# Loading W2 by row blocks and summing the left half of the first MLP's second product for three tiles at once

## The chip, the cores and the metric

The kernel runs on one core of one Trainium2 chip. The metric is the device time of one launch in microseconds (us): the median of the runs of a kernel. The profile is one execution more, recorded with its own time; the span in the profile runs from the first instruction of the program to the end of the last.

The engines are named as the profile names them: PE (matrix products; PEld its weight loads), DVE (vector work), ACT (activations), POOL (general elementwise work; it also issues the DMAs that change the type on the way) and SP (issues DMAs only).

## The reference

Attention with RMS-normed queries and keys over 8 batches, 12 heads, 448 tokens and 64 columns a head, then an MLP with LayerNorm and a residual on the joined heads. Cut to what is computed:

```python
q_n, k_n = rmsnorm(q, g_q), rmsnorm(k, g_k)              # (8, 12, 448, 64)
attn = softmax(q_n @ k_n.transpose(0, 1, 3, 2) / 8)
x = (attn @ v).transpose(0, 2, 1, 3).reshape(8, 448, 768)
xn = (x - mean(x)) / sqrt(var(x) + 1e-6) * g_ln
out = x + maximum(xn @ w_ch1, 0) @ w_ch2                 # w_ch1 (768, 3072), w_ch2 (3072, 768)
```

All inputs and the output are float32. The kernel multiplies in float16 with float32 sums.

## The kernel before

**Tiling.** Attention goes by pairs of heads (48 pairs, six a batch), each in seven steps of up to 128 keys: `scores` (L394) makes a product in PSUM and an exponential on ACT, `values` (L438) multiplies the exponentials by V. Work ahead of a pair (squares, roots, scaling, splitting K into a high and a low part, transposing) is done by `pieces` (L233) for a unit of one or two pairs. Units from `DMA_UNIT = 7` on are transposed by DMA: `dma_k` (L303) and `dma_q` (L309) on SP; the earlier ones on PE.

The MLP of batch b runs while the attention of batch b+1 does, on the same engines. `run_rest` (L976) takes the pieces of the MLP in order; each has a cost in columns, and after each piece, and after its first half, `upto` emits attention steps up to the same share of the batch's attention. So the order of instructions on each engine is fixed when the program is built: every engine works its own queue in order, and waits where an operand isn't there.

**Batch 0's MLP** is `first_mlp` (L708). The first product makes 24 row blocks of 128 hidden columns (`up`, one PSUM bank each, Relu on ACT into `hS`). The second is `down(t, g, s)`: for token tile t (three of 128 tokens), column half g of W2 (0 is the left 384 columns, 1 the right) and s from 0 to 7, three matmuls each, over row blocks 3s to 3s+2 of W2. A yield takes two values of s, so each (t, g) is four pieces of six matmuls, and the whole product 24 pieces, 144 matmuls of 128x384. A sum lives in one bank of the pool `ps_m` (tag "mlp", three banks, which the first product uses too) from s = 0 to s = 7; then `add` (L754) on DVE scales it by the LayerNorm factor and adds it to x. Before the change the order is g, then t, then s: one sum at a time.

**W2** stands in SBUF as `sh.w2[128, 24, 768]`: row block f of W2 in the second index. `load_w2(g)` (L611) fetches it on POOL's queue, float32 in memory and float16 in SBUF. Before the change g names a column half: the left half in one DMA, the right half in two DMAs of 12 row blocks each. `W2_AT = 47, 71` says at which steps of the attention they are issued. In front of the second call a POOL instruction copies one column of `kU` into `rr`, a place that `least` (L433) writes again afterwards. It reads what the transposing DMA of unit 7 writes (`dma_k`, step 70), so POOL waits for that transpose before it issues the rest of W2. The rows of V for units from 7 on (`load_v`, L207) are issued on the same queue, some between the two calls and some behind the second.

The part of `sh.w2` that row blocks 0 to 7 take holds V of batch 0 until POOL has copied it (`v_first`, L162); row blocks 12 to 23 hold nothing before W2 comes.

**After batch 0**, `weight_sums` (L760) makes differences of the quarters of W2 on DVE (L763) for the later batches. The first of them are emitted after the pieces of batch 0 of which fewer than ten are left.

Of the kernel before, what the change touches and what calls it, by code (L numbers as in the profile page):

```python
# [8 lines left out]
FP32 = mybir.dt.float32  # L9
# [7 lines left out]
ts = bass.ts  # L17
# [3 lines left out]
NDC, NFF = DM // 128, FF // 128  # L21
# [44 lines left out]
HALF, HCOL = NFF // 2, DM // 2  # L66
# [25 lines left out]
class _Fast:  # L92
# [518 lines left out]
    def load_w2(self, g):  # L611
        if g:
            self.nc.gpsimd.tensor_copy(out=self.rr[:, DMA_UNIT:DMA_UNIT + 1],
                                       in_=self.kU[DMA_UNIT % 2][:, 0:1])
        for c in (slice(0, HALF), slice(HALF, NFF)) if g else (slice(0, NFF),):
            self.nc.gpsimd.dma_start(
                out=self.sh.w2[:, c, ts(g, 384)],
                in_=self.w2[128 * c.start:128 * c.stop, ts(g, 384)].rearrange("(c p) d -> p c d", p=128))

    def tok_tiles(self, b):  # L620
        x = self.xs[b]
# [86 lines left out]
    def first_mlp(self):  # L708

        nc, sh = self.nc, self.sh  # L710
        tiles, xnT, hT, cur = self.tok_tiles(0), self.xnT, self.hS, {}

        def up(f, i):
            if i == 0:
                cur["h"] = self.ps_m.tile([128, 512], FP32, tag="mlp", name="psH")
            ps = cur["h"]
            for dc in range(3 * i, 3 * i + 3):
                nc.tensor.matmul(ps[:, 0:384], sh.w1[:, dc, ts(f, 128)], xnT[:, dc],
                                 start=(dc == 0), stop=(dc == NDC - 1))
            if i:  # L720
                nc.scalar.activation(out=hT[:, f], in_=ps[:, 0:384], func=AFT.Relu)

        def down(t, g, s):
            if s == 0:
                cur["ps"] = self.ps_m.tile([128, 512], FP32, tag="mlp", name="psC")
            ps = cur["ps"][:, 0:HCOL]
            for f in range(3 * s, 3 * s + 3):
                nc.tensor.matmul(ps, hT[:, f, ts(t, 128)], sh.w2[:, f, ts(g, HCOL)],
                                 start=(f == 0), stop=(f == NFF - 1))
            if s == 7:  # L730
                self.add(0, t, g, ps)
                if g and t < 2:
                    self.late.append((0, t, slice(0, DM)))
                elif t == 2 and not g:
                    self.late.append((0, t, slice(0, HCOL)))
                elif t == 2:
                    self.store(0, t, slice(HCOL, DM))
            elif s == 3:
                self.store_late()

        for f in range(UP_FIRST, NFF):
            yield 6 * 384 / 2.4, [lambda f=f, i=i: up(f, i) for i in range(2)]
        for g in range(2):
            for t in range(3):
                for s in range(4):
                    yield 6 * HCOL / 2.4, [lambda t=t, g=g, s=s: down(t, g, s)
                                           for s in (2 * s, 2 * s + 1)]

    def store_late(self):
        for a in self.late:  # L750
# [500 lines left out]
```

## Time and profile before

| what | us |
|---|---|
| median of 3 runs (581.79 to 582.78) | 582.78 |
| the profiled execution's own time | 579.58 |
| span of the profile | 578.0 |
| PE busy | 559.5 (97%) |
| DVE busy | 381.7 (66%) |
| ACT busy | 364.4 (63%) |
| POOL busy | 207.0 (36%) |
| first product of batch 0 on PE (L718) | starts 56.3 to 87.9 |
| second product of batch 0 on PE (L728) | starts 88.3 to 118.2 |

The profiled execution took 3.2 us less than the median of the runs, and its span is 1.6 us shorter than its time. Busy times are unions over the whole span; a row of PE shows a matmul from its issue to its modelled end, so two in a row overlap, and the distance between starts is what PE needs for one. In lists of instructions in order of time the columns are start, length, engine, line, operation, what it writes and reads, and the count of the instructions that were merged into the row; in brackets, where there is one, the idle time of the engine before it and what ended it. "q0" is the DMA queue on which POOL issues, "q1" the one on which SP does; their rows give packets, MB as landed, and the time that their packets took as a share of 16 DMA engines.

### The profile page before, as it was taken

To read this page: it belongs to the slowest core of one execution; us is meant where nothing else is said; L and a number is where in the kernel's file an instruction comes from. 1 tells how busy PE (TensorE), PEld (TensorE's weight loads), DVE (VectorE), ACT (ScalarE), POOL (GpSimd) and SP (SyncE) were. 2 spreads that over 40 slices of the span, in tenths; PEclk is the share of its full clock that TensorE was granted. 3 is DMA by queue.
4 is the path that set the end of the run, shared out by engine and by line. 5 is a ranking of instruction groups with operands and counts; after the bars stand their busy time and mean duration, and the time that the engine had idled before them with its cause. 6 is when DMAs were issued, how large, how long until landed. Compare 5 with 4: busy or idle time off the path is not lost.

```text
span 578.0 us, 13670 instructions
## 1 busy us (share of the span) xinstructions
PE 559.5 (97%) x5446; PEld 411.9 (71%) x5446; DVE 381.7 (66%) x826; ACT 364.4 (63%) x674; POOL 207.0 (36%) x224
## 2 busy tenths in 40 slices
PE   5788999999999999999999999999999999999997
PEld 4556666687686867777677768777777777878684
DVE  6989567699657586845667586854756743664424
ACT  5998787447675779557775588637777477323130
POOL 5885636404440620654241521644242320020000
PEclk9999999999999999999999999999999999999999
DMA  8999999958672876969663798958743390030201
GB/s 206 251 238 222 214 207 165 193 147 137 124 131 77 158 127 145 127 148 121 121 106 48 184 134 136 128 143 122 145 64 65 119 113 1 1 110 1 83 2 58
DMA packets 178329, 72.59 MB, mean 126 GB/s; under 512 B 138212, under 2 KB 173220, under 8 KB 178260
## 3 DMA queue, kind: packets, MB, share of 16 engines
q1 hardware_dynamic: 133876, 52.52, 44.1%
q0 software_dynamic: 43440, 18.52, 25.2%
q8 instruction: 44, 0.72, 0.5%
q10 hardware_dynamic: 944, 0.62, 0.4%
q14 instruction: 25, 0.20, 0.1%
HBM read 52.76 MB, written 11.01 MB: 110 GB/s over the span
## 4 chain that ended last, share of the span: by engine, by line
PE 77%; DVE 1%; issue 0%; DVEq 0%
PE psH L798 33%; PE psP L821 30%; PE psS L405 7%; PE oA L458 4%; PE oB L460 1%; PE psS L411 1%; DVE qn L83 0%; DVE w2s L763 0%; DVE ssq L265 0%; DVE w L763 0%; DVE xn L662 0%; DVE hS L804 0%; DVE x L475 0%; DVE xl L757 0%; DVE xl L480 0%
## 5 line engine op out<-in xcount | busy, mean ns | idle before, releaser
L421 ACT ACTIVATE E<-psS,rr_all 128x448 f16<-128x448 f32 x336 | 204.6, 634 | 47.3 <-PE psS L405 40.3
L798 PE MATMUL psH<-xnT,w 128*128 128x256 f16 (+1 forms) x2016 | 225.7, 261 | 0.0
L798 PEld LDWEIGHTS <-w 128*128 128x128 f16 x2016 | 172.8, 98 | 24.3 <-issue 4.9
L801 ACT ACTIVATE hS<-psH 128x512 f16<-128x512 f32 x150 | 89.8, 599 | 97.2 <-PE psH L798 93.0
L821 PEld LDWEIGHTS <-hS 128*128 128x128 f16 x1080 | 100.0, 98 | 57.3 <-issue 1.1
L821 PE MATMUL psP<-w,hS 128*128 128x384 f16 x672 | 127.0, 326 | 0.0
L405 PE MATMUL psS<-qU,kU 128*128 128x448 f16 x288 | 100.9, 352 | 5.0 <-ACT E L421 3.2
L458 PEld LDWEIGHTS <-E 128*128 128x128 f16 x1008 | 70.3, 98 | 35.8 <-issue 2.8
L279 POOL TENSOR_TENSOR k<-k,gprod 128x896 f32<-128x896 f32 x18 | 38.9, 2160 | 139.5 <-ACT khl L259 113.2
L804 DVE TENSOR_TENSOR hS<-hS 128x512 f16<-128x512 f16 (+1 forms) x119 | 60.2, 512 | 19.3 <-ACT hS L801 17.8
L821 PE MATMUL psP<-w2s,hS 128*128 128x384 f16 (+1 forms) x408 | 69.9, 321 | 0.0
L458 PE MATMUL oA<-v,E 128*128 128x65 f16 x864 | 66.9, 193 | 1.1 <-ACT E L421 0.6
L757 DVE SCALAR_TENSOR_TENSOR x<-psP,rs_all,x 128x384 f32<-128x384 f32 x60 | 36.4, 617 | 42.4 <-PE psP L821 41.8
L460 PE MATMUL oB<-v,E 128*128 128x65 f16 x288 | 52.0, 193 | 0.1
L832 POOL TENSOR_TENSOR x<-x,hS 128x384 f32<-128x384 f32 x21 | 23.4, 1126 | 76.1 <-ACT hS L900 75.5
L473 DVE RECIPROCAL rec_all<-oA 128x6 f32<-128x6 f32 x48 | 9.2, 193 | 53.6 <-PE oA L458 53.5
L216 POOL DMA_DIRECT2D v<-in_v_dram x54 | 41.5, 781 | 4.0 <-PE oB L460 2.7
L405 PEld LDWEIGHTS <-kU 128*128 128x128 f16 x288 | 28.0, 98 | 11.1 <-issue 2.2
L900 ACT ACTIVATE hS<-hS,rs_all 128x384 f32<-128x384 f32 x27 | 14.6, 604 | 33.0 <-DVE hS L804 33.0
L460 PEld LDWEIGHTS <-E 128*128 128x128 f16 x336 | 32.4, 96 | 0.4 <-DVE xl L480 0.3
L83 DVE SCALAR_TENSOR_TENSOR qn<-q,rr_all 128x256 f16<-128x256 f32 (+2 forms) x69 | 24.8, 420 | 7.2 <-ACT rr_all L269 7.1
L265 DVE TENSOR_REDUCE ssq<-khl 128x14 f32<-128x896 f32 (+1 forms) x24 | 25.5, 1061 | 5.0 <-ACT khl L259 4.8
(145 smaller groups left out, 616.6 us busy)
## 6 DMA issues: line engine op xcount, KB each, us to landing
k<-in_k_dram SPq DMA_DIRECT2D x19, 384.0 KB, 4.2
q<-in_q_dram SPq DMA_DIRECT2D x18, 384.0 KB, 3.9
out_dram<-x SPq DMA_DIRECT2D x14, 384.0 KB, 3.0
w<-in_moe_w_ch_dram POOLq DMA_DIRECT2D x3, 1536.0 KB, 14.3
v<-in_v_dram POOLq DMA_DIRECT2D x54, 64.0 KB, 4.4
out_dram<-x POOLq DMA_DIRECT2D x9, 384.0 KB, 2.7
w<-in_moe_w_ch_dram POOLq DMA_DIRECT2D x1, 2304.0 KB, 22.5
w<-in_moe_w_ch_dram POOLq DMA_DIRECT2D x2, 1152.0 KB, 14.4
```

The source lines that it names most:

```text
L216: nc.gpsimd.dma_start(out[:, :, j, 0:D], main[:, :, j])
L265: nc.vector.tensor_reduce(out=c["ssq"][:, n], in_=c["sq", n], axis=AX.X, op=ALU.add)
L279: (nc.vector if u in DVE_KG else nc.gpsimd).tensor_tensor(out=c["t"][1], in0=c["t"][1], in1=sh.gprod.unsqueeze(1).broadcast_to([128, g, D] ...
L405: nc.tensor.matmul(ps[0][:, 0:S], c["main"][:, ts(i, 128)], c["q"][:, ts(h, S)], start=True, stop=True)
L421: nc.scalar.activation(out=o, in_=x[:, 0:S], func=AFT.Exp, scale=self.units[u][3][:, g:g + 1], bias=EXP_BIAS)
L458: nc.tensor.matmul(oA[:, t, cs], E[:, ts(t, 128)], rhs, start=(i == 0 and t == 0), stop=(i == 6 and t == 2))
L460: nc.tensor.matmul(oB[:, cs], E[:, 320:448], rhs, start=(i == 0), stop=(i == 6))
L757: self.nc.vector.scalar_tensor_tensor(out=x, in0=ps, scalar=self.rs[:, b, t:t + 1], in1=x, op0=ALU.mult, op1=ALU.add)
L798: nc.tensor.matmul(ps[:, i], sh.w1[:, dc, ts(f + i, 128)], self.xnT[:, dc, 256 - N:256], start=(i == 0 and dc == 0), stop=(i == k - 1 and ...
L801: nc.scalar.activation(out=hT[:, f:f + k], in_=ps, func=AFT.Relu)
L804: nc.vector.tensor_tensor(out=out, in0=a, in1=c, op=op)
L821: nc.tensor.matmul(bank[x][:, c], a[:, f], w[:, f, c], start=(start and f == 0), stop=(stop and f == HALF - 1))
```

## The change

`load_w2(0)` now fetches row blocks 0 to 11 of W2 in all 768 columns, in two DMAs of six row blocks; `load_w2(1)` fetches row blocks 12 to 23 in the same way, still behind the copy that waits for unit 7's transpose. There were three DMAs and are four; the bytes are the same, and a row of a DMA is 768 columns where it was 384.

The left half (g = 0) of batch 0's second product runs with s outside and t inside: two values of s for tile 0, 1 and 2, then the next two. Three sums are open at once, so `cur` is keyed by t. The right half (g = 1) keeps its order: tile by tile, with all s for each.

```diff
-        for c in (slice(0, HALF), slice(HALF, NFF)) if g else (slice(0, NFF),):
+        for c in (0, 6) if not g else (12, 18):
             self.nc.gpsimd.dma_start(
-                out=self.sh.w2[:, c, ts(g, 384)],
-                in_=self.w2[128 * c.start:128 * c.stop, ts(g, 384)].rearrange("(c p) d -> p c d", p=128))
+                out=self.sh.w2[:, c:c + 6],
+                in_=self.w2[128 * c:128 * c + 768].rearrange("(c p) d -> p c d", p=128))
...
         def down(t, g, s):
             if s == 0:
-                cur["ps"] = self.ps_m.tile([128, 512], FP32, tag="mlp", name="psC")
-            ps = cur["ps"][:, 0:HCOL]
+                cur[t] = self.ps_m.tile([128, 512], FP32, tag="mlp", name="psC")
+            ps = cur[t][:, 0:HCOL]
...
-        for g in range(2):
-            for t in range(3):
-                for s in range(4):
-                    yield 6 * HCOL / 2.4, [lambda t=t, g=g, s=s: down(t, g, s)
-                                           for s in (2 * s, 2 * s + 1)]
+        for g, s, t in ([(0, s, t) for s in range(4) for t in range(3)]
+                        + [(1, s, t) for t in range(3) for s in range(4)]):
+            yield 6 * HCOL / 2.4, [lambda t=t, g=g, s=s: down(t, g, s)
+                                   for s in (2 * s, 2 * s + 1)]
```

## The prediction

> **What bounds the kernel now.** I read the page first, then the PE waits, then PE's and POOL's rows in order of time around batch 0's second product, then the DMA queues in short windows. The page's chain of waits, by engine:
>
> ```profile
> PE 77%; DVE 1%; issue 0%; DVEq 0%
> ```
>
> PE holds most of the chain. The view of who waited for whom, PE alone, from 60 us to the end, lists two waits and nothing else:
>
> ```profile
> PE tr L382 <- DVE kU L373: 0.3, 1, 0.3
> PE psS L405 <- ACT E L421: 0.3, 1, 0.3
> ```
>
> One late stretch in the busy-time view (length, then PE, PEld, DVE, ACT, POOL busy, granted clock, DMA share, GB/s):
>
> ```profile
> 200.00:400.00 200.00, 200.00 (x1967) 149.43 (x1966) 134.95 (x297) 137.33 (x253) 78.84 (x84) 1.00 0.81 130
> ```
>
> So after 60 us PE has no slack worth naming, and a wait put into PE there moves the end by its own length: nothing later can give it back. The change acts between 61 and 118 us. What PE does there, from the rows in order of time (start, length, line, count):
>
> ```profile
> 88.33 0.65 PE L728 MATMUL psC<-w,hS 128*128 128x384 f16 x3
> ...
> 97.58 1.14 PE L728 MATMUL psC<-w,hS 128*128 128x384 f16 x6
> ...
> 100.74 1.14 PE L728 MATMUL psC<-w,hS 128*128 128x384 f16 x6
> ```
>
> L728 is the second product: 24 pieces of 6 matmuls, one every 0.163 us when nothing is between. Counting the rows from 88.33, piece 7 begins with the first matmul at 97.58, piece 10 with the fourth at 100.74 (101.23), piece 13 at 105.5, and piece 15 at 108.6 (in a row of 66 matmuls that starts at 107.62). Before, piece 13 is the first to read the right half of W2. When W2 comes, from POOL's rows:
>
> ```profile
> 61.42 1.51 POOL L616 DMA_DIRECT2D w<-in_moe_w_ch_dram  x1
> ...
> 87.33 0.18 POOL L613 CAST rr_all<-kU 128x1 f32<-128x1 f16 x1 [8.04 <-DMA kU<-khl]
> 87.57 2.09 POOL L616 DMA_DIRECT2D w<-in_moe_w_ch_dram  x2
> ```
>
> and L616's times from issue to landing (min, median, max of three):
>
> ```profile
> DMA to landing us min/median/max: 10.9/17.8/22.5
> ```
>
> The 22.5 is the whole left half: 83.9, 4.4 us ahead of 88.33. The 10.9 belongs to the DMA issued at 87.57 (landed 98.5), the 17.8 to the one some 1.03 later (106.4). Before, those are rows 0-11 of the right half, wanted at 105.5, and rows 12-23, wanted at piece 15 (108.6): 7 and 2.2 us to spare. The gate in front of them is L613, which copies one column of unit 7's transposed K and so waits for that transpose.
>
> **The change, part by part.**
>
> *PE's work*: 144 matmuls of the same shape and as many weight loads, the same yields, the same order of attention between them: 0. *Order*: the left half now runs through row blocks 0-5 for three tiles, then 6-11, 12-17, 18-23. Blocks 12-17 are therefore wanted at piece 7 (97.58) and 18-23 at piece 10 (101.23). They are the two DMAs behind the gate. With the old landings (98.5 and 106.4) PE would wait 0.9 us, then until 106.4: 5.2 us in all. What is left of this depends on how much sooner whole rows land.
>
> *Rows of 1536 landed bytes for 768.* Packets, MB and share of each queue, in 98.5 to 101 us, where the W2 queue is alone; in 101 to 104, where SP's q and k loads run beside it; and in 44 to 48, where W1, whose rows land as 2048 bytes, runs beside SP's loads:
>
> ```profile
> q0 software_dynamic: 655, 0.50, 131.9%
> ```
> ```profile
> q0 software_dynamic: 468, 0.36, 76.1%
> q1 hardware_dynamic: 442, 0.34, 45.1%
> ```
> ```profile
> q0 software_dynamic: 321, 0.66, 86.3%
> q1 hardware_dynamic: 323, 0.25, 24.6%
> ```
>
> Shared, the queues go row for row whatever the sizes (468 to 442, 321 to 323), so a wider row takes a larger share. A pair of rows costs an engine 16 x 3/468 = 0.103 us with 768, 16 x 4/321 = 0.199 with 2048; on the line between them 0.161 with 1536: 0.153 MB/us where it had 0.36/3 = 0.120. Alone, 655 rows in 2.5 us are 0.201 MB/us; for wider rows the bounds are that (no gain) and, with the same slope, 0.061 + 0.058 = 0.119 us a row, 0.206 MB/us. I take 0.206, for W1's pair has the slope in it; it hardly matters.
>
> [...]
>
> *The gate.* Unit 7's transpose is issued at 80.69 behind its last operand on DVE, not behind a load, and landed 6.6 us later. Its line, over all units:
>
> ```profile
> DMA to landing us min/median/max: 4.0/5.6/8.0
> ```
>
> W2's first load should be through sooner: between 66 and 80 us the W2 queue moved 2273 rows beside 2269 on SP's queue. So unit 7's small V rows, behind it, clear the engines before the transpose's packets come. Bounds for the gate: 87.33 as now, and 80.69 + 4.0 = 84.7. I take the median, 86.3: 1.0 us sooner.
>
> *The two DMAs behind it*, 1.18 MB each. Before: 1410 rows by 97 us, 1045 more by 101. The first DMA's 1536 rows were through at 97.5, and it landed 1.0 later; the last 617 at 156 per us were through at 104.95, and it landed 1.45 later. From 92 to 97.2 it ran at 1056/5.2 = 203 rows per us, not 262, beside SP's transposes: 1.2 us lost, of which wide rows win back between 0 and all; I take 0.6. After: first DMA through at 97.5 - 1.0 - 0.6 = 95.9, landed 96.9: piece 7 doesn't wait, with 0.7 us to spare. Second: alone to 101.0, 5.1 x 0.206 = 1.05 MB, the other 0.13 at 0.153 takes 0.85, so 101.85 + 1.45 = 103.3. Piece 10 waits 103.3 - 101.2 = **2.1 us**. Late end: gate unmoved, nothing won back, 0.201: 3.5 us alone, 0.70 MB, 0.48/0.153 = 3.1, landed 105.55, stall 4.3. Early end: gate 84.7, all 1.2 won: landed before 101.2, stall 0.
>
> *POOL's issues.* 3072 rows cost 1.51 us, 1536 rows 1.03: 0.81 each for 768 on that line, at most 1.06. First load 1.62 for 1.51, second 1.62 for 2.09. Behind the first stand unit 6's casts and L290, and then POOL idles 3.8 us until 73.78: 0, and 0.1 to 0.6 if somebody waited for those casts; nobody does in the view of waits. SP issues nothing new; its q and k loads land a little later, wanted by ACT at 105.6 at the soonest.
>
> *Three sums at once* take all three banks of the pool psH used. The third sum's bank is freed by ACT's last Relu (88.22 + 0.49), its piece comes near 91. Adds (0.62 each on DVE) move from 94, 101 and 105.7 to about 105 to 107, where DVE was idle; the right half's first sum wants the first bank two pieces later. 0; without that cover 0.6 per add. Weight sums (L763) start at 111.64 as before, plus the stall.
>
> **Sum.** Everything is 0 but the stall: span 578.0 + 2.1 = 580.1; this execution 579.6 + 2.1 = 581.7. It lies 3.2 below the median of the runs, so the forecast goes on the median: 582.8 + 2.1 = **584.9**.
>
> **Rivals.**
>
> *Whole rows arrive in time.* It decides from a landing of the fourth DMA at 102.4 or sooner (stall under 1.2). For it: the gate could come 2.6 us sooner, and each microsecond of it moves up to 0.206 MB out of the stretch that SP's loads share, which is worth 1.3 us of landing. Against: the median of L306 gives 1.0 only. Time 582.8, 582.8 to 584.0. Chance 0.20, of which 0.06 ends below by scatter (the runs shown span 1.0 us).
>
> *Wide rows bring nothing.* The fourth DMA lands at 106.4 as now: stall 5.2, time 588.0. For it: alone the queue may be limited by bytes, 0.201 against 0.206. Against: the row-for-row sharing. PE's clock then matters. At the end PE idles with the clock still granted:
>
> ```profile
> 574.20:578.00 3.80, 0.00 (x0) 0.00 (x0) 0.42 (x1) 0.00 (x0) 0.00 (x0) 1.00 0.51 159
> ```
>
> so 3.8 us idle cost nothing. Cold, the same warm-up matmul ran at half speed:
>
> ```profile
> 5.98 2.74 PE L532 MATMUL psW<-id 128*128 128x128 f16 x24
> ...
> 9.29 0.72 PE L532 MATMUL psW<-id 128*128 128x128 f16 x10
> ```
>
> from 2.74 to about 8.7 us, so a fall costs at most 3.0 more: 588 to 591. Chance 0.13. [...]
>
> *A bank isn't free.* The adds queue up on DVE and PE waits for a bank at piece 13: up to 3 x 0.62 = 1.9 more, 586.8. Chance 0.03; DVE is busy 0.5 of 4.3 us there.
>
> **The numbers.** Forecast, stall 1.2 to 4.3 (584.0 to 587.1): 0.64. Faster or slower by over 0.2% (1.2 us) is what a measurement here can tell from none: faster 0.06, same 0.14, slower 0.64 + 0.13 + 0.03 = 0.80. Range 582.4 to 588.6: it holds the forecast, most of the first rival and the plain 5.2 us stall, and leaves out the fall of the clock.
>
> **What would show it.** PE's L728 with an idle of about 2 us before one matmul near 101 to 103.5, released by a DMA of w; no wait at piece 7; L613 near 86.3; W2's third and fourth DMA landing near 97 and 103.3; PE unbroken after it. No such wait on L728 means the first rival; a landing at 106 the second; a stall with an unmoved span would break the premise that PE has no slack.

## The result and the profile after

| | before | after |
|---|---|---|
| median of 10 runs, us | 581.89 | 584.96 |
| runs, us | 581.58 to 582.78 | 582.58 to 586.74 |
| ratio, 95% interval | | 1.0048 [1.0033, 1.0063] |
| the profiled execution's own time, us | 579.58 | 585.00 |
| span of the profile, us | 578.0 | 583.5 |

The change makes the kernel 3.1 us slower by the medians (1.9 to 3.7 by the interval of the ratio), and the runs scatter some three and a half times as widely. One of the ten runs after was a slow one (834.94 us, at a granted clock of 0.66 where the others have 0.995 or more); it is left out of the ratio and of the range above, and without it the median is 584.93.

The page's chain of waits, by engine, after:

```profile
PE 81%; DMA 15%; SPq 1%; POOL 1%; DVE 0%; issue 0%; ACTq 0%; DVEq 0%
```

Before, the chain went back only to 123 us, behind the second product, so it said nothing of this stretch. Now it goes back further: at the wait it leaves PE for the loads, and DMAs hold a seventh of the span. The waits of PE from 60 us on (what waited, for what: us in total, times, the longest):

```profile
PE psC L728 <- DMA w<-in_moe_w_ch_dram: 2.0, 1, 2.0
PE tr L382 <- DVE kU L373: 0.3, 1, 0.3
PE psS L405 <- ACT E L421: 0.3, 1, 0.3
```

The two old waits are there unchanged and one is new: the second product, for W2. Where it stands, from PE's rows in order of time:

```profile
97.98 1.14 PE L728 MATMUL psC<-w,hS 128*128 128x384 f16 x6
...
101.14 0.65 PE L728 MATMUL psC<-w,hS 128*128 128x384 f16 x3
103.79 0.65 PE L728 MATMUL psC<-w,hS 128*128 128x384 f16 x3 [2.00 <-DMA w<-in_moe_w_ch_dram]
...
106.47 1.82 PE L728 MATMUL psC<-w,hS 128*128 128x384 f16 x6
```

Piece 7 (97.98) doesn't wait. The row at 101.14 ends piece 9, the one at 103.79 begins piece 10, the first to read row block 18. The last row matters too: six matmuls took 1.82 us where the row at 97.98 shows 1.14. The busy-time view by stretches (length, PE, PEld, DVE, ACT, POOL busy, granted clock, DMA share, GB/s) tells why:

```profile
101.05:104.46 3.41, 1.41 (x9) 0.68 (x7) 0.35 (x2) 0.63 (x1) 0.00 (x0) 1.00 1.30 221
104.46:107.87 3.41, 3.41 (x22) 2.00 (x21) 0.62 (x1) 1.27 (x2) 0.00 (x0) 0.50 1.49 203
107.87:111.28 3.41, 3.41 (x34) 2.16 (x32) 1.69 (x3) 2.59 (x5) 0.40 (x1) 1.00 0.67 113
```

For 3.41 us behind the wait PE had half its clock: 22 matmuls where the next stretch of the same length has 34.

The new loads, from POOL's rows:

```profile
61.83 1.75 POOL L616 DMA_DIRECT2D w<-in_moe_w_ch_dram  x2
...
86.01 0.18 POOL L613 CAST rr_all<-kU 128x1 f32<-128x1 f16 x1 [6.30 <-DMA kU<-khl]
86.24 1.70 POOL L616 DMA_DIRECT2D w<-in_moe_w_ch_dram  x2
```

and L616's time from issue to landing, for the DMA issued at 86.24 and for the one at 87.1:

```profile
DMA to landing us min/median/max: 11.0/11.0/11.0
```
```profile
DMA to landing us min/median/max: 16.6/16.6/16.6
```

They land at 97.3 and 103.7: PE starts again as the fourth DMA lands. The spans differ by 5.4 us, and three places make it up. PE reaches the second product 0.4 us later (88.73 for 88.33), ahead of all that the change touches. From there to the first matmul of batch 1's MLP (118.36 before, 122.57 after) it loses 3.8: 2.0 idle and some 1.8 at the half clock and in restarting. After it the distance stays 4.2 to PE's last matmul; the remaining 1.2 lies behind that, in the last stores, which took 3.9 us before and 5.1 after (5.5 in the kernel with the order alone, below, which has no such wait). Between profiles only the 3.8 belongs to the change.

### The profile page after: what moved, and what is told of

Its sections match the earlier page's. It is cut to its first block, busy times and chain, and to the rows that moved or that the text cites. A ratio compares the mean times of both kernels' runs of the same rounds, so it can differ in the third digit from the quotient of the medians.

```text
span 583.5 us, 13670 instructions
## 1 busy us (share of the span) xinstructions
PE 561.3 (96%) x5446; PEld 412.8 (71%) x5446; DVE 382.3 (66%) x826; ACT 363.7 (62%) x674; POOL 206.9 (35%) x225
## 4 chain that ended last, share of the span: by engine, by line
PE 81%; DMA 15%; SPq 1%; POOL 1%; DVE 0%; issue 0%; ACTq 0%; DVEq 0%
PE psH L797 34%; PE psP L820 30%; PE psS L405 7%; PE oA L458 5%; DMA w2s<-in_v_dram 4%; DMA k<-in_k_dram 3%; DMA w<-in_moe_w_ch_dram 3%; PE psC L728 3%; DMA q<-in_q_dram 2%; PE oB L460 2%; PE psS L411 2%; DMA hS<-in_k_dram 1%; DMA w<-in_v_dram 1%; DMA kU<-khl 1%; SPq L146 1%; DMA w2s<-in_k_dram 1%
## 5 line engine op out<-in xcount | busy, mean ns | idle before, releaser
L800 ACT ACTIVATE hS<-psH 128x512 f16<-128x512 f32 x150 | 89.8, 599 | 97.2 <-PE psH L797 93.1
L728 PE MATMUL psC<-w,hS 128*128 128x384 f16 x144 | 27.7, 336 | 2.0 <-DMA w<-in_moe_w_ch_dram 2.0
```

The source lines that it names most:

```text
L800: nc.scalar.activation(out=hT[:, f:f + k], in_=ps, func=AFT.Relu)
```

## The experiments

**One part alone.** First the order without the loads: W2 by column halves as before.

```diff
-        for c in (0, 6) if not g else (12, 18):
+        for c in (slice(0, HALF), slice(HALF, NFF)) if g else (slice(0, NFF),):
             self.nc.gpsimd.dma_start(
-                out=self.sh.w2[:, c:c + 6],
+                out=self.sh.w2[:, c, ts(g, 384)],
...
```

> W2 loaded by column halves as before, the left half summed for three tiles at once as after. Theory (the loss is a wait for row blocks 12 to 23 of W2, which whole rows bring too late): the left half has landed near 84 us, ahead of 88.3, so L728 shows no wait on a DMA, the clock stays at 1.00 and the time is that of before within 0.2%. Rival (three open sums cost by themselves, in banks or in adds): still 2 to 4 us slower than before.

581.73 us against 581.62, ratio 1.0003 [0.9993, 1.0014], no wait on L728. Three open sums, their banks and their adds cost nothing that this measurement can tell from none.

Then the loads without the order: whole rows, and the second product tile by tile as before.

```diff
-        for g, s, t in ([(0, s, t) for s in range(4) for t in range(3)]
-                        + [(1, s, t) for t in range(3) for s in range(4)]):
+        for g in range(2):
+            for t in range(3):
+                for s in range(4):
...
```

> W2 loaded by whole rows as after, the second product tile by tile as before. Theory: blocks 12 to 17 are wanted at the third piece of the first tile (about 92.5 us) and land near 97, blocks 18 to 23 one piece later and land near 103.7. PE waits some 4.7 and then 5 us, about 10 in all, and loses up to 1.7 us more for each fall of the clock: 10 to 14 us slower than before. Rival (the loads have nothing to do with it): 2 to 4 us slower, as the full change.

593.26 us, the median of two runs, ratio 1.0203 [1.0179, 1.0227]: 11.6 slower. PE's rows with a wait of some length:

```profile
97.74 2.08 PE L728 MATMUL psC<-w,hS 128*128 128x384 f16 x6 [4.90 <-DMA w<-in_moe_w_ch_dram]
...
103.58 2.08 PE L728 MATMUL psC<-w,hS 128*128 128x384 f16 x6 [3.39 <-DMA w<-in_moe_w_ch_dram]
```

Both waits are where they were expected, 8.3 us in all for the 9.7 expected; the second is shorter mainly because PE did the pieces between at half clock (0.50 from 97.05 to 107.29). So whole rows make the loss, and the new order takes three quarters of it away again. It does not take all.

**Which bytes come first.** Row blocks 0 to 11 by whole rows; 12 to 23 by column halves, the left one first.

```diff
-        for c in (0, 6) if not g else (12, 18):
+        if not g:
+            for c in (0, 6):
...
+            return
+        for h in range(2):
             self.nc.gpsimd.dma_start(
-                out=self.sh.w2[:, c:c + 6],
-                in_=self.w2[128 * c:128 * c + 768].rearrange("(c p) d -> p c d", p=128))
+                out=self.sh.w2[:, HALF:NFF, ts(h, 384)],
+                in_=self.w2[128 * HALF:128 * NFF, ts(h, 384)].rearrange("(c p) d -> p c d", p=128))
```

> Row blocks 0 to 11 by whole rows as after, blocks 12 to 23 by column halves as before, left half first, behind the same gate. Theory (it counts which bytes come first): all that pieces 7 to 12 want comes with the third DMA, which lands near 97.5 us, against 98.0 for the first need; a wait of 0 to 0.5 us, no fall of the clock, time of before within 0.2%. Rival (row width decides): as slow as the full change, since the second load's rows are narrow again.

581.93 us, ratio 1.0009 [0.9995, 1.0023], no wait. The third DMA landed at 98.51 (piece 7 began at 98.55 in that execution), the fourth at 106.24. With the left half of those blocks in the third DMA nobody wants the fourth until piece 15. The cause is what the fourth DMA holds, not when it lands.

**Row width.** The same bytes ahead of what is wanted, in narrow rows: each DMA cut into two by columns, right half first.

```diff
-        for c in (0, 6) if not g else (12, 18):
+        for c, h in ((0, 1), (0, 0), (6, 1), (6, 0)) if not g else ((12, 1), (12, 0), (18, 1), (18, 0)):
             self.nc.gpsimd.dma_start(
-                out=self.sh.w2[:, c:c + 6],
+                out=self.sh.w2[:, c:c + 6, ts(h, 384)],
...
```

> The full change with each DMA of W2 cut into two by columns, right half first, so rows are 384 columns wide again while the same bytes stand ahead of what is wanted. Theory (wide rows take a larger share beside SP's loads): row block 18 lands 2 to 3 us later than in the full change, at 105.5 to 106.5, PE waits 4 to 5 us, and with the fall of the clock it is 6 to 8 us slower than before. Rival (the width is of no account): the wait of the full change, 2 us.

588.13 us over four runs, ratio 1.0115 [1.0095, 1.0135]: 6.6 slower, inside what was expected, with a fall of the clock (0.50 from 105.65 to 109.07), but with a wait of 3.6 us where 4 to 5 were expected. So the mechanism is weaker than the time says. This kernel also has twice as many DMAs, which was not tried apart. Its last DMA landed at 105.64, 18.3 us behind the first issue of the second load; in four executions of the full change that was 17.5, 18.2, 17.9 and 17.6. Rows twice as wide brought the last byte 0.1 to 0.8 us sooner. The row-for-row sharing and both rates did hold in the stretches counted. Packets and MB of the full change in 97 to 100 us, W2 alone, and in 100.5 to 102, beside SP's loads:

```profile
q0 software_dynamic: 406, 0.62, 114.7%
```
```profile
q0 software_dynamic: 146, 0.22, 81.5%
q1 hardware_dynamic: 146, 0.11, 29.8%
```

0.207 and 0.147 MB/us, where 0.206 and 0.153 had been worked out. The counts are equal over a short time too: in 0.2 us of the profile before (45.2 to 45.4), with W1 beside SP's loads, there are 16 rows of each queue. What failed to come is the gain in the slow stretch before it: the third DMA took 11.0 us where the narrow one took 10.9.

**The gate.** The full change without the copy that waits for unit 7's transpose.

```diff
-        if g:
-            self.nc.gpsimd.tensor_copy(out=self.rr[:, DMA_UNIT:DMA_UNIT + 1],
-                                       in_=self.kU[DMA_UNIT % 2][:, 0:1])
```

> The full change without the copy on POOL that waits for unit 7's transpose, so the third and fourth DMA of W2 are issued near 80 us in place of 86. Theory: they land near 90 and 96 us, ahead of 98.0 and 101.6; no wait on L728, no fall of the clock, time of before within 0.3%. Rival (the gate shields the transposes of unit 7 and what follows): these land late and somebody waits for them, 1 us or more slower than before.

587.36 us over four runs, ratio 1.0090 [1.0064, 1.0115]: my theory fell and the rival held. The profile shows the slowest of the four, 590.87 us. In it W2 no longer makes PE wait, unit 7's transposes of Q do. PE's row, and SP's issues:

```profile
107.19 0.53 PE L405 MATMUL psS<-qU,kU 128*128 128x448 f16 x1 [6.07 <-DMA qU<-qn]
```
```profile
81.09 9.19 SPq L306 DMA_TRANSPOSE kU<-khl  x1
90.40 9.35 SPq L312 DMA_TRANSPOSE qU<-qn  x3
```

SP was 2.55 and 3.82 us over these two rows in the full change. The queues between 88 and 96 us say why:

```profile
q0 software_dynamic: 804, 1.21, 93.6%
q1 hardware_dynamic: 803, 0.21, 23.8%
```

One row for one row again, and here that hurts: a row of W2 lands 1536 bytes, a row of a transpose 256. Over these 8 us the transposes got 0.21 MB beside W2's 1.21, about a sixth.

**Only the third DMA ahead of the gate.**

```diff
-        for c in (0, 6) if not g else (12, 18):
+        for c in (0, 6, 12) if not g else (18,):
```

> The full change with the third DMA (row blocks 12 to 17) issued right behind the first two, ahead of the gate; the fourth stays behind it. Theory (a row of W2 for a row of a transpose): 768 more wide rows run beside unit 7's transpose of K, which lands 4 to 5 us later, near 91; the fourth DMA then lands near 100 to 101.5, by itself, against 101.6, and Q's transposes near 98, against 101.1. A wait of 0 to 1 us, time 0 to 1.5 us over before. Rival (any load ahead of the gate costs what taking the gate away cost): 5 to 6 us over before, with the wait at the first scores of unit 7.

582.60 us, ratio 1.0019 [1.0000, 1.0038], runs from 581.18 to 586.37, three of ten near 586. The median is inside the theory's range, the profile isn't: it shows one of the 586 us executions, with the transpose of K landed at 95.7 (91 expected), the fourth DMA issued at 96.02, landed at 105.2, and a wait of 3.5 us. What the seven faster runs had in place of this was not seen.

**Smaller DMAs.** The second load in four DMAs of three row blocks.

```diff
-        for c in (0, 6) if not g else (12, 18):
+        for c, n in ((0, 6), (6, 6)) if not g else ((12, 3), (15, 3), (18, 3), (21, 3)):
             self.nc.gpsimd.dma_start(
-                out=self.sh.w2[:, c:c + 6],
-                in_=self.w2[128 * c:128 * c + 768].rearrange("(c p) d -> p c d", p=128))
+                out=self.sh.w2[:, c:c + n],
+                in_=self.w2[128 * c:128 * c + 128 * n].rearrange("(c p) d -> p c d", p=128))
```

> The full change with the third and fourth DMA of W2 cut into two each, three row blocks at a time, behind the same gate. Theory (PE waits for bytes that it doesn't yet need): row blocks 18 to 20 land 2 to 3 us ahead of 21 to 23, near 101.5 to 103; the one wait becomes two short ones of 1.5 us or less in all, no window of 3.4 us holds 2 us of idle, so the clock holds, and the time is 1 to 2 us over before, 1 to 2 under the full change. Rival (the end of the load decides, since 21 to 23 are wanted 0.7 us after 18): the same wait and the same time as the full change.

583.25 us, ratio 1.0032 [1.0017, 1.0047]: 1.5 over before, by the medians half of what the change loses. The interval overlaps those of the full change (1.0033 to 1.0063 and, below, 1.0030 to 1.0069), so that it gains over the full change is likely, not shown. Row blocks 18 to 20 landed at 100.1, in time; 21 to 23 at 103.52, so one short wait is left where two were expected:

```profile
100.67 1.14 PE L728 MATMUL psC<-w,hS 128*128 128x384 f16 x6
...
103.56 0.65 PE L728 MATMUL psC<-w,hS 128*128 128x384 f16 x3 [1.32 <-DMA w<-in_moe_w_ch_dram]
```

**The clock.** The full change again, beside two kernels that fill PE's wait with 34 or 17 small matmuls into unused columns of a bank.

```diff
             ps = cur[t][:, 0:HCOL]
+            if (g, s, t) == (0, 6, 0):
+                for _ in range(34):
+                    nc.tensor.matmul(cur[t][:, HCOL:512], self.sh.id16, self.sh.id16,
+                                     start=False, stop=False)
```

> The full change once more, beside the next three on one chip. Expected: 2.5 to 4 us slower than before, a wait of about 2.0 us at L728 for W2, and then 3.4 us of granted clock 0.50.

> The full change with 34 small matmuls of 128 columns, about 1.9 us of PE, into an unused part of a bank just ahead of the first matmul that needs row block 18. They stand where PE would idle. Theory (2.0 us of wait plus 1.7 us of half clock behind it): the clock stays at 1.00, the wait shrinks to 0.3 us or less, and the time is about 1.5 us under the full change, some 2 us over before. Rival (the loss is the wait alone, the low clock in the profile is of no account): the same as the full change.

> As the last, with 17 small matmuls: PE idles about 1.1 us ahead of row block 18. It asks how long an idle the clock stands. Before, an idle of 1.41 us at 17 us went by with no fall. Theory (a fall wants between 1.4 and 2.0 us of idle): no fall, the time of the kernel with 34. Rival (any idle in the wrong place of a window does it): a fall in some runs, time between that kernel and the full change.

The full change: 584.75 us, ratio 1.0050 [1.0030, 1.0069]. With 34: 585.56, 1.0060 [1.0042, 1.0078]. With 17: 585.89, 1.0066 [1.0052, 1.0080]. The expected gain didn't come. In the profile with 34 the clock did stay at 1.00, but PE still waited 1.4 us (0.3 or less expected); with 17 it waited 2.0 us (1.1 expected) and the clock fell (0.50 from 105.98 to 109.39). A likely reason is that the fillers are paid in every run while the landing moves: the full change's runs go from 582.1 to 587.0, and the fastest with 34 fillers is 583.7. As a measure of the clock these two kernels failed. The new trace of the full change was worth more. PE waited twice:

```profile
98.99 1.14 PE L728 MATMUL psC<-w,hS 128*128 128x384 f16 x6 [0.89 <-DMA w<-in_moe_w_ch_dram]
105.88 0.65 PE L728 MATMUL psC<-w,hS 128*128 128x384 f16 x3 [3.08 <-DMA w<-in_moe_w_ch_dram]
```

3.1 us idle and no fall, where 2.0 us had brought one in the first profile. The trace gives the times at which the granted clock changes; in each execution they lie whole multiples of 3.41 us apart (at 104.46, 107.87 and 582.33 in the first profile of the full change, 1 and 139 steps). Cut by that grid, this wait falls into two windows (busy times by stretches, columns as above):

```profile
100.55:103.97 3.42, 2.25 (x17) 1.30 (x15) 1.23 (x4) 1.06 (x2) 0.00 (x0) 1.00 1.13 227
103.97:107.38 3.41, 1.50 (x16) 1.01 (x16) 0.00 (x0) 0.62 (x1) 0.00 (x0) 1.00 1.37 225
```

1.17 and 1.91 us idle. So I formed a rule (a fall wants about 2 us of idle in one window) and traced the full change twice more.

> The full change once more, for its trace. What the clock did so far (a fall behind 2.0 us of idle in one execution, none behind 3.1 in another) is read as a rule: the granted clock changes only at steps of 3.41 us from its other changes, and it falls where about 2 us or more of one such window are idle. Expected: a wait of 0.5 to 4 us for W2 at piece 10, by the landing of the fourth DMA; a fall if its idle has 2.0 us or more in one window of that grid, none if the grid cuts it into less.

> As the last run, one execution more, with the same rule for the clock.

585.48 and 583.56 us, one run each. The first waited 0.6 and 2.7 us, cut by the grid into 1.30 and 1.44 at most (the view of waits names a load of q for the 2.7, but the fourth DMA of W2 landed at 105.1 and PE went on at 105.15); the second 2.2 us, cut into 1.78 and 0.38; no fall in either. All executions with a wait on this stretch, by the most idle in one window of their grid:

| execution | longest wait, us | most idle in a window, us | fall |
|---|---|---|---|
| smaller DMAs | 1.3 | 1.32 | no |
| 34 fillers | 1.4 | 1.39 | no |
| full change, third | 2.7 | 1.44 | no |
| full change, fourth | 2.2 | 1.78 | no |
| third DMA ahead | 3.5 | 1.79 | no |
| full change, second | 3.1 | 1.91 | no |
| full change, first | 2.0 | 2.00 | yes |
| 17 fillers | 2.0 | 2.03 | yes |
| narrow rows | 3.6 | 3.41 | yes |
| no gate | 6.1 | 3.41 | yes |
| loads alone | 4.9 | 3.41 | yes |

The length of the wait doesn't sort this table; the window does, between 1.91 and 2.00. But the rule doesn't hold outside it. Near their start four of this case's traces show a fall behind less idle: 1.51 us (full change, fourth), 1.53 (third DMA ahead), 1.70 (loads alone) and 1.93 (which bytes come first). The first of them, cut by its grid:

```profile
11.13:14.54 3.41, 1.90 (x16) 0.87 (x14) 3.21 (x4) 2.56 (x6) 2.77 (x3) 1.00 1.13 256
14.54:17.96 3.42, 3.42 (x26) 2.84 (x27) 3.42 (x4) 2.28 (x5) 3.28 (x4) 0.50 1.11 331
```

In that one execution 1.51 us of idle brought a fall and, at 99.88, 1.78 us did not. So idle time by these rows, in which the ends of matmuls are modelled, is not what decides alone; what does stays open.

## Why the prediction came out as it did

**Place, direction and cause: as predicted, and shown.** PE has no slack after 60 us (0.3 us twice is all that it waits there in the profile before), so the wait reaches the end whole. It stands at piece 10, for the fourth DMA, in each of the four traced executions; piece 7 didn't wait in two of them, as forecast, and waited 0.9 and 0.6 us in the others. That the loss comes of which bytes stand in the last DMA is shown by changing one thing at a time. The order costs nothing alone, the same order with the left half first costs nothing, the rows alone cost 11.6 us.

**The time: 584.9 us forecast, 584.96 measured. So close a hit is luck.** The forecast stood on 582.8, the median of three runs; over ten runs the kernel before takes 581.89. The loss is 3.1 us, not 2.1. An estimate from the four traced executions: a mean wait of 2.9 us, and 1.7 us for the clock in one of the four, 0.4 on the mean, are 3.3.

**The wait: 2.1 us forecast, 2.0 in the profile.** That nearness hides two errors. In this execution the gate opened at 86.0 (86.3 forecast) and the fourth DMA landed at 103.7 (103.3), while PE came 0.4 later to piece 10. Over the four traced executions the wait, piece 7's included, was 2.0, 4.0, 3.3 and 2.2 us, 2.9 on the mean. The mis-sized term is what wide rows win back from the slow stretch between 92 and 97 us: I took 0.6 of 1.2 us, and the third DMA's 11.0 to 11.4 us against 10.9 show none of it. The other is the gate's scatter: 86.0 and 85.8 in two executions, 87.4 and 87.0 in the others, which sets the wait at 2.0 and 2.2 or at 4.0 and 3.3. In the first two, W2's second DMA had landed by 80.7 us and unit 7's transpose of K took 4.9 and 5.0 us; in the others W2 landed at 81.7 to 81.9 and the transpose took 6.0 and 6.3. That the load of W2 ahead of it makes the difference fits, and was not tried by itself.

**The clock: missed.** I read 3.8 us of idle at the very end, with the clock still granted, as a stretch of idle that costs nothing, and gave the fall to the 5.2 us rival alone. That row had no matmul behind it, and it ended too soon: in the trace before the clock falls at 578.66, 0.6 us past the end of the span, and in the profile after it is 0.50 from 582.33 on, inside the span. Idle time by its length was the wrong measure too. In the first profile the fall cost some 1.7 us: of 3.41 us at half clock, half is lost. It came once in four executions of the full change, and by the table above that hangs on how the grid cuts the wait. A window didn't have to be idle whole: 2.00 us of one, and near the start 1.51, stood before a fall. The 3.0 us at most for a fall were an estimate from PE's rows near the start; in both of them, 5.98 to 8.72 and 9.29 to 10.01 us, the granted clock is 1.00, so they show no fall of it.

**The rivals.** Whole rows in time: no execution traced, though the runs near 582.3 come close. Wide rows bring nothing: nearly so for the last byte (0.1 to 0.8 us), but the gate and the wide rows' share beside SP's loads (0.147 MB/us, where the narrow rows before had 0.36 MB in 3 us, 0.120) kept the wait under 5.2. A bank that isn't free: ruled out by the order alone. The range was wide enough for the scatter: each of the nine runs in the table's range lies in it.

**POOL's issues:** 1.75 us for the first two against 1.62 worked out, nobody waiting.

No version tried here beats the kernel before: PE is busy for 97% of its span, and from 60 us on it doesn't wait for W2 there.

## What to carry to other kernels

When a load is recut, ask for each piece of the consumer which DMA brings its last byte: here a cut by rows put a quarter of the wanted half into the last DMA, and a loop order that spread the need out bought back three quarters of it. If a PE-bound stage must wait, a finer cut of the load at the place of the wait is worth trying: here its profile has a wait of 1.3 us, where those of the full change have 2.0 to 4.0, though the gain in time is not clear of the scatter. Wide rows are no free gift to whoever shares the queues: without the gate 804 rows of W2 went beside 803 of unit 7's transposes, and PE waited 6.07 us for these. A gate in front of a big load may be there for the small transfers behind it.

## What the runs showed of the hardware

In four stretches with both DMA queues at work their counts of rows came out equal or nearly so: 468 to 442 at 768 bytes each (before, 101 to 104 us), 321 of 2048 to 323, 0.25 MB in all (before, 44 to 48), 146 of 1536 to 146 of 768 (full change, 100.5 to 102), 804 of W2's 1536 to 803 of SP's, 0.21 MB in all (no gate, 88 to 96). In 92 to 97.2 of the profile before, W2's narrow rows beside SP's transposes, they did not: 1056 to 309. The transposes of one unit, 16 us from first issue to last landing in the full change's profile (81.1 to 97.0), kept PE waiting until 107.2 in the kernel without the gate.

The granted clock changed at times whole multiples of 3.41 us apart, and the grid lay elsewhere from one execution to the next (a change at 104.46 in the first profile of the full change, at 105.98 with 17 fillers). Where PE waited for W2 or for the transposes, it halved after windows with 2.00 us or more of PE idle and not after those with 1.91 or less; near the start it fell after as little as 1.51, so neither figure is a threshold. It came back after windows with 0.03 us of idle at most (narrow rows, 105.65 to 109.07) and stayed low after one with 0.96 (loads alone, 97.05 to 100.46). By estimate, half of 3.41, one such fall costs some 1.7 us, and in the kernel without the gate, where idle ran on into the next window, it lasted 6.8 us.
